# Two norms' row sums in one reciprocal: a windowed attention kernel on one Trainium2 core

## The chip, the cores and the metric

The kernel runs on one core of a Trainium2 chip. That core has a matrix engine (TensorE, PE in the profile), a vector engine (VectorE, DVE), an activation engine (ScalarE, ACT), a general engine (GpSimd, POOL) and SyncE (SP), which here only issues DMAs. The engines run at the same time and wait for one another through semaphores; each takes its own instructions in order. Matmuls write to PSUM, from which VectorE or ScalarE copy the result to SBUF. The metric is the device time of one execution in microseconds (us), and the median over several is compared.

## The reference

Two independent attention layers, A and B, of the same shape: 2048 tokens, width 1024, 32 heads of 32. Each query sees the 256 keys up to and including its own.

```python
def _A_ref(x, wqkv, wo):
    B, S, D = x.shape
    H = 32; Dh = D // H; W = 256
    qkv = (x @ wqkv).reshape(B, S, 3, H, Dh).transpose(2, 0, 3, 1, 4)
    q, k, v = qkv[0], qkv[1], qkv[2]
    scores = jnp.einsum("bhqd,bhkd->bhqk", q, k) * (Dh ** -0.5)
    idx = jnp.arange(S)
    mask = (idx[:, None] - idx[None, :] >= 0) & (idx[:, None] - idx[None, :] < W)
    p = softmax(jnp.where(mask[None, None], scores, -1e9), axis=-1)
    o = jnp.einsum("bhqk,bhkd->bhqd", p, v)
    return o.transpose(0, 2, 1, 3).reshape(B, S, D) @ wo
...
return jnp.concatenate([a, b], axis=-1)
```

All data are bf16 outside, sums are float32.

## The kernel before

**Tiling.** Tokens are cut into 16 blocks of 128 and 4 chunks of 512. Heads are taken in groups of four (128 columns), so there are 8 groups per problem and 16 in all, numbered `g`. For a key block j only the query blocks j, j+1 and j+2 matter, which makes 45 block pairs in a group. The list of all 16 x 45 pairs is cut into 180 *sessions* of four (L421).

**A session.** TensorE computes the transposed scores of four block pairs for four heads into one PSUM tile `st` (L434: four matmuls on 32-row tiles of the array at the same time). ACT takes one exponential over 128x2048 elements (L442) into `pt`. POOL zeroes the masked halves of the first and the last of the three blocks of a query (L450, L454). There is one `st`, so scores of the next session wait for the exponential.

**P·V and the norm.** For each group and each pair p of query blocks (8 per group, 128 in all) `pv` (L469) multiplies the exponentials with v and, with a matrix of ones, sums them over the keys. Four heads run beside each other on 32-column tiles of the array. Everything goes into one PSUM bank `acc` of 128 x 2 x 256 float32: half 0 is the product for two query blocks, half 1 the row sums, each repeated on the 32 rows of its head. For p > 0 VectorE has first added the two masked `pt` blocks of each query block into `both` (`edge`, L464), which saves row-sum matmuls: one burst of four 256-wide matmuls covers both query blocks' edges. The norm is three VectorE instructions that lie in the list `side`: two reciprocals of 128x128 (L505) and a multiplication of 128x256 (L510) that writes bf16 into `oT`. `acc` has two buffers.

**Projections.** `qk_steps`, `v_steps` and `out_steps` make *chains* of matmuls over eight 128-row tiles (`ct`) into one of two PSUM tiles `pp`, evacuated by ACT or VectorE (`evacuate`, L188). A chain of 8 or 16 matmuls has an earliest session (`early`), set among others by when its data are expected (`landed`), and a latest one (`late`). After the scores and the P·V of a session, `emit` issues steps of chains up to a budget that `level` spreads evenly over the sessions to come. Around P·V the projections run as four 32-column matmuls (L176) instead of one of 128 (L172), which spares a change of the array's tiling.

**Planner.** All this order is written out at build time. `_Clock` keeps estimated times of PE, ACT and VectorE; `COST` holds the estimates in ns with which `evacuate` chooses an engine and `emit` decides when to issue a piece of a norm. PE's order doesn't depend on `COST`.

**Loads.** Later weights and the x chunks of problem B are cut into pieces (L279 to L324). In each session, after a POOL mask that precedes it, a piece's destination is touched by a POOL memset of one column (L334) and its DMA issued on SP. A chunk of x comes in eight transposing DMAs of 128 tokens by 512 columns (L133). `arrival` records the session from which data count as there: that of the last piece plus two. For problem B, chunk k=2 is asked for from session 79, k=3 from 82; B's first scores are in session 90.

**Start.** The first 512 tokens come as four plain row loads on SP (L526), are transposed on PE (`flip`, L557) and copied by ACT and VectorE; the weights of q and k for group 0 are issued on ACT's queue (L528). POOL copies at L529 and L532 read row block 2 and write a column of `wv` and of x chunk 1, so those two loads on SP wait until that row block is in. Then come the weights of group 1, x chunks 2 and 3, and `wv` for groups 2 and 3.

**End.** The last output chain is evacuated 288 columns by ACT and 224 by VectorE, each with a DMA of its own (L257 to L260).

Of the kernel before, what the change touches and what calls it, by code (L numbers as in the profile page):

```python
# [8 lines left out]
BF16 = mybir.dt.bfloat16  # L9
F32 = mybir.dt.float32  # L10
# [3 lines left out]
ALU = mybir.AluOpType  # L14
# [4 lines left out]
P = 128  # L19
# [7 lines left out]
QB = 4  # L27
SLOTS = 4
VG = 2
NS_MM = 216.0  # L30
# [3 lines left out]
PV_LAG = 3  # L34
FREE = 10 ** 6
ACT_EXP = 1800.0
COST = {"act": 590.0, "dve": 670.0, "or": 560.0, "rinv": 930.0, "mult": 430.0,
        "edge": 340.0}


class _Cfg:
# [37 lines left out]
def _fast_path(ctx, tc, cfg, problems, outs, consts, certify):  # L79
    nc = tc.nc  # L80
# [30 lines left out]
    vp = ctx.enter_context(tc.tile_pool(name="vt", bufs=2 * NQ))  # L111
    ptp = ctx.enter_context(tc.tile_pool(name="pt", bufs=7))
    edgep = ctx.enter_context(tc.tile_pool(name="edge", bufs=2))
    misc = ctx.enter_context(tc.tile_pool(name="misc", bufs=2))
    osbp = ctx.enter_context(tc.tile_pool(name="osb", bufs=4))
    once = ctx.enter_context(tc.tile_pool(name="once", bufs=1))
    ps_st = ctx.enter_context(tc.tile_pool(name="ps_st", bufs=1, space=PSUM))
# [30 lines left out]
    def new_wv(m):  # L148
        wv[m] = wvp.tile([P, CT, VG * P], BF16, name="wv")
# [38 lines left out]
    def evacuate(out, in_, engines=("act", "dve")):  # L188
        if clock.evacuate(engines) == "act":
            nc.scalar.copy(out=out, in_=in_)  # L190
        else:
            nc.vector.tensor_copy(out=out, in_=in_)  # L192
# [23 lines left out]
    def v_steps(m, b):  # L216
# [19 lines left out]
                steps.append((NS_MM * w_ / 512.0, f))  # L236
        return steps

    def out_steps(pi, b, ch):
        k, a = divmod(b, QB)  # L240
        st_ = {}
        steps = []
        for ct in range(CT):
            def f(ct=ct):
                if ct == 0:
                    st_["pp"] = new_pp()
                by_columns(st_["pp"], 0, 512, oTs[(pi, k)][:, ct, a * P:(a + 1) * P],
                           wo_sb[(pi, ch)][:, ct, :], ct == 0, ct == CT - 1)
                clock.pe += NS_MM
                if ct == CT - 1:  # L250
                    osb = osbp.tile([P, 512], BF16, name="osb")
                    dst = outs[pi][b * P:(b + 1) * P, ch * 512:(ch + 1) * 512]
                    if chains or current:
                        evacuate(osb[:], st_["pp"][:])
                        nc.sync.dma_start(out=dst, in_=osb[:])
                    else:
                        nc.scalar.copy(out=osb[:, 0:288], in_=st_["pp"][:, 0:288])  # L257
                        nc.vector.tensor_copy(out=osb[:, 288:512], in_=st_["pp"][:, 288:512])
                        nc.scalar.dma_start(out=dst[:, 0:288], in_=osb[:, 0:288])
                        nc.sync.dma_start(out=dst[:, 288:512], in_=osb[:, 288:512])  # L260
            steps.append((NS_MM, f))
        return steps

# [45 lines left out]
    def entries_of(now):  # L309
        return [(n // NE,) + entries[n % NE]  # L310
                for n in range(now * SLOTS, min((now + 1) * SLOTS, G * NE))]

    pieces = {}
    arrival = {}
    free = 0
    for time, key, fs in wanted:
        free = max(free, time)
        new = fs[0]
        for where, f in fs[1:]:
            while len(pieces.get(free, [])) >= sum(q != j + 1 for _, j, q in entries_of(free)):  # L320
                free += 1
            pieces.setdefault(free, []).append((new, where, f))
            new = None
        arrival[key] = free + 2  # L324
# [29 lines left out]
    for pi in range(NPROB):  # L354
        final = pi == NPROB - 1
        for b in range(NB):
            k = b // QB
            for ch in range(cfg.NCH):
                early = max(pv_time(pi * T + T - 1, 2 * k + 1) + 1, landed("wo", pi, ch))
                late = FREE if final else wo_time[(pi + 1, ch)] - 1  # L360
                if not final and k < NPROB * NQ - (2 * NQ - 1):
                    late = pv_time((pi + 1) * T, 2 * (2 * NQ - 1 - NQ + k)) - 1
                chains.append(_Chain(early, late, out_steps(pi, b, ch)))
    assert all(c.early <= c.late for c in chains), [(c.early, c.late, c.size) for c in chains
                                                    if c.early > c.late]
    chains.sort(key=lambda c: c.late)
# [102 lines left out]
    def pv(g, p):  # L469
        pi, t = divmod(g, T)  # L470
        m, u = divmod(g, VG)
        k, h = divmod(p, QB // 2)
        segs = []
        for j in range(max(2 * p - 2, 0), 2 * p + 2):
            for q in range(max(j, 2 * p), min(j + 3, 2 * p + 2)):
                s, a = place(g, j, q)
                if segs and segs[-1][0] == j and segs[-1][2] == s:
                    segs[-1][4] += 1
                else:
                    segs.append([j, q, s, a, 1])  # L480
        acc = ps_acc.tile([P, 2, 256], F32, name="acc")
        clock.pe = max(clock.pe, clock.norms.pop(0))
        moves = [(0, j, (q - 2 * p) * P, n * P, pts[s][:, :, a:a + n, :])
                 for (j, q, s, a, n) in segs]
        for (j, q, s, a, n) in segs:
            for i in range(n):
                if p == 0 or q + i == j + 1:
                    moves.append((1, j, (q + i - 2 * p) * P, P, pts[s][:, :, a + i:a + i + 1, :]))
        if p:
            moves.append((1, 0, 0, 2 * P, edges.pop((g, p))))  # L490
        for x, (which, j, o, w_, src) in enumerate(moves):
            for r in range(4):
                c = u * P + 32 * r
                lhsT = ones[:, 0:32] if which else vts[(m, j // QB)][:, j % QB, c:c + 32]
                nc.tensor.matmul(acc[32 * r:32 * r + 32, which, o:o + w_], lhsT=lhsT,  # L495
                                 rhs=src[:, r, :, :], start=(x == 0), stop=(x == len(moves) - 1),
                                 tile_position=(0, 32 * r), skip_group_check=True)
            clock.pe += NS_PV * w_ / P
        if (pi, k) not in oTs:
            oTs[(pi, k)] = opool.tile([P, T, 512], BF16, name="oT")  # L500
        rinv = misc.tile([P, 256], F32, name="rinv")
        pieces = []
        for a in range(2):
            def f(a=a):
                nc.vector.reciprocal(out=rinv[:, a * P:(a + 1) * P],  # L505
                                     in_=acc[:, 1, a * P:(a + 1) * P])
            pieces.append((COST["rinv"], f, False))

        def f():
            nc.vector.tensor_tensor(out=oTs[(pi, k)][:, t, h * 256:(h + 1) * 256],  # L510
                                    in0=acc[:, 0, :], in1=rinv[:], op=ALU.mult)
        pieces.append((COST["mult"], f, True))
        n = max([i + 1 for i, x in enumerate(side) if x[2]], default=0)
        side[n:n] = pieces
# [7 lines left out]
    new_wqk(0)  # L522
    new_wv(0)
    xrow = [rows[:, 2 * a:2 * a + 2, :].rearrange("p t n -> p (t n)") for a in range(QB)]
    for a in range(QB):
        nc.sync.dma_start(out=xrow[a], in_=problems[0][0][a * P:(a + 1) * P, :])  # L526
    for which in range(2):
        load_wqk(0, which, nc.scalar)  # L528
    nc.gpsimd.tensor_copy(out=wv[0][:, 0, 0:1], in_=xrow[2][:, 0:1])  # L529
    load_wv(0, 0, CT, nc.sync)  # L530
    new_x(0, 1)
    nc.gpsimd.tensor_copy(out=xT[(0, 1)][:, 0, 0:1], in_=xrow[2][:, 0:1])  # L532
    load_x(0, 1)
    new_wqk(1)
    for which in range(2):
# [1 line left out]
    for k in range(2, NQ):  # L537
        new_x(0, k)
        load_x(0, k)
    new_wv(1)  # L540
    load_wv(1, 0, CT, nc.sync)

    warm = ps_proj.tile([P, 512], F32, name="pp")
    for _ in range(5):
        nc.tensor.matmul(warm[:], lhsT=blank[:, 0:P], rhs=blank[:, 0:512], start=True, stop=True)
    flips = [ps_acc.tile([P, 2, 256], F32, name="acc") for _ in range(2)]
    flips = [f[:].rearrange("p a q -> p (a q)") for f in flips]
    flips.append(ps_st.tile([P, 4, SLOTS, P], F32, name="st")[:, 0].rearrange("p a q -> p (a q)"))
    flips.append(None)
    held = [{}, {}]  # L550

    def flip(a):
        if a == 3:
            flips[a] = ps_acc.tile([P, 2, 256], F32, name="acc")[:].rearrange("p a q -> p (a q)")
        f = flips[a].bitcast(BF16).rearrange("p (ct q) -> p ct q", q=P)
        for ct in range(CT):
            nc.tensor.transpose(out=f[:, ct, :], in_=xrow[a][:, ct * P:(ct + 1) * P],  # L557
                                identity=ident[:])
        dst = xT[(0, 0)][:, :, a * P:(a + 1) * P]
        half = CT // 2  # L560
        nc.scalar.copy(out=dst[:, :half, :], in_=f[:, :half, :])
        nc.vector.tensor_copy(out=dst[:, half:, :], in_=f[:, half:, :])
# [170 lines left out]
def kernel(  # L733
# [16 lines left out]
    outs = [of[:, pi * D:(pi + 1) * D] for pi in range(len(problems))]  # L750

    cpool = ctx.enter_context(tc.tile_pool(name="consts", bufs=1))
    ones = cpool.tile([P, 32], BF16, name="ones")
    nc.vector.memset(ones[:], 1.0)
    ones1 = cpool.tile([P, 1], F32, name="ones1")
    nc.vector.memset(ones1[:], 1.0)
    pm = cpool.tile([P, 1], F32, name="pm")
# [65 lines left out]
```

## Time and profile before

| | |
|---|---|
| median of 8 executions | 617.99 us (612.51 to 620.76) |
| the profiled execution | 617.02 us |
| its span in the profile | 615.3 us |
| the largest groups: exponentials on ACT (L442) | 180 x 1878 ns |
| masks on POOL (L450, L454) | 480 x some 690 ns |
| edge adds on DVE (L464) | 224 x 628 ns |
| matmuls of PE: L176, L172, L495, L434 | 6156, 1037, 3696, 1488 |
| DMA moved | 35.4 MB, mean 58 GB/s |

The span runs from the first to the last instruction in the profile; the time of an execution holds a little around it (1.7 us here). In the profile, "busy" of PE is the union of matmul records whose ends are modelled, so the starts of matmuls say more than their lengths. An entry such as "<-PE acc L495 29.4" gives idle time of an engine and who ended it. PEclk is the granted clock of TensorE in tenths.

### The profile page before, as it was taken

Reading aid. Unit: us, or ns where it says so; the run is one execution under the profiler, and the core shown is the slowest. Engines: PE = TensorE matmul, PEld = TensorE weight load, DVE = VectorE, ACT = ScalarE, POOL = GpSimd, SP = SyncE. Lnnn points to the kernel's source line nnn. Section 1 sums busy time; section 2 is a strip of 40 time slices with the busy share of each in tenths; the row PEclk is TensorE's granted clock in tenths of the full one; section 3 lists DMA queues with packets and bytes.
Section 4 is the critical chain, followed back from the end, with each engine's and each line's share of the span. In section 5 each row is a group of like instructions: output and inputs, shape, how many; then the busy total and the mean of one; then the engine's idle time right before and its main releaser. Section 6 shows DMA issues by size and latency. Waiting matters only on the chain.

```text
span 615.3 us, 27586 instructions
## 1 busy us (share of the span) xinstructions
PE 600.7 (98%) x12416; PEld 343.9 (56%) x12416; DVE 507.9 (83%) x817; ACT 440.7 (72%) x372; POOL 321.8 (52%) x632
## 2 busy tenths in 40 slices
PE   7999999999999999989999999999999999999996
PEld 5465466556655656545556665745446564545442
DVE  1488989998999899969998999888998999899300
ACT  3677888788878888748777777777777778775332
POOL 0456665655566666536555556556556555555000
PEclk9999999999999999989999999999999999999999
DMA  8924110111004510534101010112012030114221
GB/s 205 206 64 113 38 37 3 36 38 38 3 20 96 110 25 8 84 86 107 37 14 37 27 38 2 37 37 79 12 31 61 2 107 20 54 45 131 69 78 64
DMA packets 86796, 35.40 MB, mean 58 GB/s; under 512 B 65680, under 2 KB 86160, under 8 KB 86672
## 3 DMA queue, kind: packets, MB, share of 16 engines
q1 hardware_dynamic: 84448, 32.97, 21.6%
q8 instruction: 99, 1.62, 1.1%
q10 hardware_dynamic: 2224, 0.60, 0.4%
q14 instruction: 25, 0.20, 0.1%
HBM read 17.83 MB, written 8.39 MB: 43 GB/s over the span
## 4 chain that ended last, share of the span: by engine, by line
PE 91%; DMA 3%; DVE 2%; SPq 1%; ACT 1%; issue 0%; POOL 0%; DVEq 0%; ACTq 0%
PE pp L176 42%; PE pp L172 27%; PE acc L495 13%; PE st L434 9%; DMA xT<-in_A_x_dram 1%; DMA oT<-in_A_x_dram 1%; SPq L133 1%; ACT pt L442 1%; DVE rinv L505 1%; DVE both L464 1%; DMA xT<-in_B_x_dram 0%; DVE top L184 0%; SPq L145 0%; SPq L526 0%; DVE osb L192 0%
## 5 line engine op out<-in xcount | busy, mean ns | idle before, releaser
L442 ACT ACTIVATE pt<-st 128x2048 bf16<-128x2048 f32 x180 | 338.1, 1878 | 80.3 <-PE st L434 63.6
L505 DVE RECIPROCAL rinv<-acc 128x128 f32<-128x128 f32 x256 | 227.1, 924 | 29.7 <-PE acc L495 29.4
L454 POOL TENSOR_SCALAR_AFFINE_SELECT pt<-pt 128x512 bf16<-128x512 bf16 x224 | 151.8, 678 | 148.7 <-ACT pt L442 148.7
L450 POOL TENSOR_SCALAR_AFFINE_SELECT pt<-pt 128x512 bf16<-128x512 bf16 x256 | 177.4, 694 | 87.7 <-ACT pt L442 86.9
L176 PE MATMUL pp<-xT,wqk 128*32 128x512 bf16 x2688 | 160.5, 379 | 0.0
L464 DVE TENSOR_TENSOR both<-pt 128x512 bf16<-128x512 bf16 x224 | 131.7, 628 | 0.0
L176 PEld LDWEIGHTS <-wqk 128*32 128x32 bf16 x2688 | 71.5, 97 | 54.9
L172 PE MATMUL pp<-xT,wqk 128*128 128x512 bf16 (+1 forms) x368 | 86.7, 380 | 5.1 <-POOL wv L334 3.2
L176 PE MATMUL pp<-wv,xT 128*32 128x256 bf16 x2548 | 78.6, 273 | 0.0
L434 PE MATMUL st<-qT,kT 32*128 32x384 bf16 (+2 forms) x1488 | 71.6, 269 | 0.0
L176 PEld LDWEIGHTS <-xT 128*32 128x32 bf16 x2548 | 68.2, 97 | 4.6
L495 PE MATMUL acc<-pt,vt 128*32 128x128 bf16 (+1 forms) x2160 | 63.3, 239 | 0.1
L172 PE MATMUL pp<-wo_sb,oT 128*128 128x512 bf16 x282 | 63.1, 379 | 0.0
L434 PEld LDWEIGHTS <-kT 32*128 32x128 bf16 x1488 | 22.2, 92 | 66.1 <-issue 65.6
L172 PEld LDWEIGHTS <-wqk 128*128 128x128 bf16 x368 | 34.5, 100 | 43.9 <-issue 13.6
L510 DVE TENSOR_TENSOR oT<-acc,rinv 128x256 bf16<-128x256 f32 x128 | 54.1, 423 | 3.7
L190 ACT CAST osb<-pp 128x512 bf16<-128x512 f32 x51 | 29.8, 585 | 38.1 <-PE pp L172 25.7
L176 PE MATMUL pp<-wo_sb,oT 128*32 128x512 bf16 x920 | 54.0, 379 | 0.0
L495 PEld LDWEIGHTS <-vt 128*32 128x32 bf16 x2160 | 35.9, 96 | 26.6 <-issue 24.7
L172 PE MATMUL pp<-wv,xT 128*128 128x256 bf16 x387 | 47.3, 273 | 0.3 <-ACT kT L190 0.2
L172 PEld LDWEIGHTS <-oT 128*128 128x128 bf16 x282 | 26.9, 98 | 32.6 <-issue 1.7
L190 ACT CAST qT<-pp 128x512 bf16<-128x512 f32 x47 | 27.5, 584 | 21.5 <-PE pp L172 11.1
(46 smaller groups left out, 363.7 us busy)
## 6 DMA issues: line engine op xcount, KB each, us to landing
out_dram<-osb SPq DMA_DIRECT2D x63, 128.0 KB, 1.7
wqk<-in_B_wqkv_dram SPq DMA_DIRECT2D x32, 128.0 KB, 2.7
wqk<-in_A_wqkv_dram SPq DMA_DIRECT2D x24, 128.0 KB, 2.6
wo_sb<-in_A_wo_dram SPq DMA_DIRECT2D x16, 128.0 KB, 2.2
wv<-in_B_wqkv_dram SPq DMA_DIRECT2D x16, 128.0 KB, 2.5
wo_sb<-in_B_wo_dram SPq DMA_DIRECT2D x16, 128.0 KB, 2.3
oT<-in_A_x_dram SPq DMA_DIRECT2D x4, 256.0 KB, 5.1
wv<-in_A_wqkv_dram SPq DMA_DIRECT2D x2, 512.0 KB, 4.0
```

Of the source, the lines that this page charges most:

```text
L133: nc.sync.dma_start_transpose(out=xT[(pi, k)][:, c0:c1, lo:hi], in_=problems[pi][0][k * 512 + lo:k * 512 + hi, c0 * P:c1 * P])
L172: nc.tensor.matmul(out[:, lo:hi], lhsT=lhsT, rhs=rhs, start=start, stop=stop, skip_group_check=True)
L176: nc.tensor.matmul(out[c:c + 32, lo:hi], lhsT=lhsT[:, c:c + 32], rhs=rhs, start=start, stop=stop, tile_position=(0, c), skip_group_check=True)
L190: nc.scalar.copy(out=out, in_=in_)
L434: nc.tensor.matmul(st[:, r, a:b, :], lhsT=kT[32 * r:32 * r + 32, j * P:(j + 1) * P], rhs=qT[32 * r:32 * r + 32, q * P:(q + b - a) * P], st ...
L442: nc.scalar.activation(out=pt[:, :, :n, :].rearrange("p r a q -> p r (a q)"), in_=st[:, :, :n, :].rearrange("p r a q -> p r (a q)"), func= ...
L450: nc.gpsimd.affine_select(out=blk, in_=blk, pattern=[[0, 4], [1, P]], compare_op=ALU.is_ge, fill=0.0, base=0, channel_multiplier=-1)
L454: nc.gpsimd.affine_select(out=blk, in_=blk, pattern=[[0, 4], [-1, P]], compare_op=ALU.is_gt, fill=0.0, base=0, channel_multiplier=1)
L464: nc.vector.tensor_tensor(out=both[:, :, h, :], in0=pts[s0][:, :, a0, :], in1=pts[s1][:, :, a1, :], op=ALU.add)
L495: nc.tensor.matmul(acc[32 * r:32 * r + 32, which, o:o + w_], lhsT=lhsT, rhs=src[:, r, :, :], start=(x == 0), stop=(x == len(moves) - 1), t ...
L505: nc.vector.reciprocal(out=rinv[:, a * P:(a + 1) * P], in_=acc[:, 1, a * P:(a + 1) * P])
L510: nc.vector.tensor_tensor(out=oTs[(pi, k)][:, t, h * 256:(h + 1) * 256], in0=acc[:, 0, :], in1=rinv[:], op=ALU.mult)
```

## The change

1. **Row sums stacked.** `ones` becomes two 128x32 matrices: the first has ones in columns 0 to 15, the second in 16 to 31, zeros elsewhere. The sums of the pair's first query block then land on rows 0 to 15 of each head's 32, those of the second on 16 to 31, in the same 128 columns. `acc` is 128x512, of which 384 columns are used. The burst on `both` is split in two, one for each query block.
2. **The norm.** One reciprocal of 128x128; then two stream shuffles that copy row 0 or row 16 of each 32 to all 32 rows, into the two halves of `wide`; then the multiplication as before, with `wide`. Shuffles and multiplication are one piece. `rinv` and `wide` have one buffer each.
3. **Planner.** `COST` of "mult" and "edge" is raised. Of an x chunk at most two pieces go into a session. The loads of the start are entered in `arrival`: x chunks 2 and 3 count from sessions 3 and 5, q/k weights of group 1 from 1, `wv` of groups 2 and 3 from 4.
4. **First loads.** On SP: row blocks 0 and 1, k's weights, row blocks 2 and 3, `wv`, x chunk 1, and so on; q's weights alone stay on ACT's queue. Both POOL copies go. The second `wv` is issued ahead of x chunk 3.
5. **End.** The last chain is computed and stored in two halves of 256 columns, each in its own `pp` and with one evacuation and one DMA on SP.

```diff
-COST = {... "rinv": 930.0, "mult": 430.0, "edge": 340.0}
+COST = {... "rinv": 930.0, "mult": 900.0, "edge": 620.0}
...
-    misc = ctx.enter_context(tc.tile_pool(name="misc", bufs=2))
+    normp = ctx.enter_context(tc.tile_pool(name="norm", bufs=1))
...
+    def store(pi, b, ch, lo, hi, pp):
+        osb = osbp.tile([P, 512], BF16, name="osb")
+        evacuate(osb[:, lo:hi], pp[:, lo:hi])
+        nc.sync.dma_start(out=outs[pi][b * P:(b + 1) * P, ch * 512 + lo:ch * 512 + hi],
+                          in_=osb[:, lo:hi])
+
+    def last_steps(pi, b, ch):
...
+        for lo in (0, 256):
+            for ct in range(CT):
+                def f(ct=ct, lo=lo):
+                    if ct == 0:
+                        st_["pp"] = new_pp()
+                    by_columns(st_["pp"], lo, lo + 256, oTs[(pi, k)][:, ct, a * P:(a + 1) * P],
+                               wo_sb[(pi, ch)][:, ct, lo:lo + 256], ct == 0, ct == CT - 1)
+                    clock.pe += NS_MM / 2
+                    if ct == CT - 1:
+                        store(pi, b, ch, lo, lo + 256, st_["pp"])
...
-                    osb = osbp.tile([P, 512], BF16, name="osb")
-                    dst = outs[pi][b * P:(b + 1) * P, ch * 512:(ch + 1) * 512]
-                    if chains or current:
-                        evacuate(osb[:], st_["pp"][:])
-                        nc.sync.dma_start(out=dst, in_=osb[:])
-                    else:
-                        nc.scalar.copy(out=osb[:, 0:288], in_=st_["pp"][:, 0:288])
-                        nc.vector.tensor_copy(out=osb[:, 288:512], in_=st_["pp"][:, 288:512])
-                        nc.scalar.dma_start(out=dst[:, 0:288], in_=osb[:, 0:288])
-                        nc.sync.dma_start(out=dst[:, 288:512], in_=osb[:, 288:512])
+                    store(pi, b, ch, 0, 512, st_["pp"])
...
-    arrival = {}
+    arrival = {("x", 0, k): t for k, t in ((2, 3), (3, 5))}
+    arrival.update({("wqk", 1): 1, ("wv", 1): 4})
...
-            while len(pieces.get(free, [])) >= sum(q != j + 1 for _, j, q in entries_of(free)):
+            while len(pieces.get(free, [])) >= min(2 if key[0] == "x" else SLOTS, sum(
+                    q != j + 1 for _, j, q in entries_of(free))):
                 free += 1
...
-        acc = ps_acc.tile([P, 2, 256], F32, name="acc")
+        acc = ps_acc.tile([P, 512], F32, name="acc")
...
                 if p == 0 or q + i == j + 1:
-                    moves.append((1, j, (q + i - 2 * p) * P, P, pts[s][:, :, a + i:a + i + 1, :]))
+                    moves.append((q + i - 2 * p, j, 2 * P, P, pts[s][:, :, a + i:a + i + 1, :]))
         if p:
-            moves.append((1, 0, 0, 2 * P, edges.pop((g, p))))
+            both = edges.pop((g, p))
+            moves += [(h, 0, 2 * P, P, both[:, :, h:h + 1, :]) for h in range(2)]
...
-                lhsT = ones[:, 0:32] if which else vts[(m, j // QB)][:, j % QB, c:c + 32]
+                lhsT = vts[(m, j // QB)][:, j % QB, c:c + 32] if h is None else ones[:, h, :]
...
-        for a in range(2):
-            def f(a=a):
-                nc.vector.reciprocal(out=rinv[:, a * P:(a + 1) * P],
-                                     in_=acc[:, 1, a * P:(a + 1) * P])
-            pieces.append((COST["rinv"], f, False))
 
         def f():
-            nc.vector.tensor_tensor(out=oTs[(pi, k)][:, t, h * 256:(h + 1) * 256],
-                                    in0=acc[:, 0, :], in1=rinv[:], op=ALU.mult)
+            nc.vector.reciprocal(out=rinv[:], in_=acc[:, 2 * P:3 * P])
+        pieces.append((COST["rinv"], f, False))
+
+        def f():
+            for h in range(2):
+                nc.vector.stream_shuffle(out=wide[:, h * P:(h + 1) * P], in_=rinv[:],
+                                         mask=[16 * h] * 32)
+            nc.vector.tensor_tensor(out=oTs[(pi, k)][:, t, (p % 2) * 256:(p % 2 + 1) * 256],
+                                    in0=acc[:, 0:256], in1=wide[:], op=ALU.mult)
         pieces.append((COST["mult"], f, True))
...
+    load_wqk(0, 0, nc.scalar)
     for a in range(QB):
         nc.sync.dma_start(out=xrow[a], in_=problems[0][0][a * P:(a + 1) * P, :])
-    for which in range(2):
-        load_wqk(0, which, nc.scalar)
-    nc.gpsimd.tensor_copy(out=wv[0][:, 0, 0:1], in_=xrow[2][:, 0:1])
+        if a == 1:
+            load_wqk(0, 1, nc.sync)
     load_wv(0, 0, CT, nc.sync)
     new_x(0, 1)
-    nc.gpsimd.tensor_copy(out=xT[(0, 1)][:, 0, 0:1], in_=xrow[2][:, 0:1])
     load_x(0, 1)
...
         load_x(0, k)
-    new_wv(1)
-    load_wv(1, 0, CT, nc.sync)
+        if k == 2:
+            new_wv(1)
+            load_wv(1, 0, CT, nc.sync)
...
-    ones = cpool.tile([P, 32], BF16, name="ones")
-    nc.vector.memset(ones[:], 1.0)
+    ones = cpool.tile([P, 2, 32], BF16, name="ones")
+    nc.vector.memset(ones[:], 0.0)
+    nc.vector.memset(ones[:, 0, 0:16], 1.0)
+    nc.vector.memset(ones[:, 1, 16:32], 1.0)
```

## The prediction

> **What bounds the kernel now.** I read the page first: span, busy shares, the slices, the chain.
>
> ```profile
> span 615.3 us, 27586 instructions
> PE 600.7 (98%) x12416; PEld 343.9 (56%) x12416; DVE 507.9 (83%) x817; ACT 440.7 (72%) x372; POOL 321.8 (52%) x632
> ...
> PEclk9999999999999999989999999999999999999999
> ...
> PE 91%; DMA 3%; DVE 2%; SPq 1%; ACT 1%; issue 0%; POOL 0%; DVEq 0%; ACTq 0%
> ```
>
> TensorE is busy or on the chain nearly always, at full clock but for one slice. Busy time alone doesn't prove it streams, so I took the starts of all its matmuls and compared each spacing with columns/2.4 ns plus a few ns. All excess together is 44.5 us: 37 us are pauses of 0.1 us where the shape of the array tile changes (two per session, not touched by the change); most of the rest lies at three places below. Seven other spacings of 0.14 to 0.35 us over sum to 1.6 us.
>
> VectorE is the engine to be relieved. The table of windows, for the stretch in which norms run (its columns: window, us, then busy us of PE, PEld, DVE, ACT, POOL), then the groups and the waits:
>
> ```profile
> 25.00:576.00 551.00, 546.88 (x12117) 316.02 (x12116) 501.69 (x802) 418.20 (x341) 316.67 (x618) 1.00 0.20 50
> L505 DVE RECIPROCAL rinv<-acc 128x128 f32<-128x128 f32 x256 | 227.1, 924 | 29.7 <-PE acc L495 29.4
> L510 DVE TENSOR_TENSOR oT<-acc,rinv 128x256 bf16<-128x256 f32 x128 | 54.1, 423 | 3.7
> PEld L495 <- DVE oT L510: 0.6, 2, 0.3
> ```
>
> VectorE is 91% busy there, but it is VectorE that waits for PE (29.4 us), while PE waits for a norm 0.6 us in all. Work taken from VectorE is work taken from an engine that is not last.
>
> **Norms on VectorE.** Removed: one reciprocal in each of 128 norms, 924 ns. Added: two shuffles of 128x128 f32 with a mask that alternates. The trace has no shuffle. Nearest row is L510: 423 ns for 256 elements, of which 256/0.96 = 267 ns stream (one element a cycle, if the clock is the 0.96 GHz of the Trainium skill's "Trainium Kernel Development and Optimization", NeuronCore Architecture), leaving 156 ns fixed. So 128 elements: 133 + 156 = 290 ns. The skill's "VectorE: DVE Perf Modes", The perf-mode tier table, gives about 2400 ns for 2048 elements with no faster mode, hence 267 ns fixed and 400 ns here; no run here shows one. Loading the mask has no row: between 0 and 0.15 us, an estimate (one more fixed part). Ends: 290 to 550 ns per shuffle. I take 350, by the row it is nearest to: 2x350 - 924 = -224 ns per norm, 29 us off VectorE (ends: -44 and +23 us). The same skill page, Rules for kernel authors, says to minimize the count of chained operations, which speaks against trading one for two; by row or rule the new pair costs about or under the old reciprocal. **To the span: nothing** in any of these cases, since PE's streaming hides it. That cover ends where the pair exceeds 924 ns plus the slack per norm, (551 - 502)/128 = 385 ns: at 0.65 us each.
>
> The norm's pieces go from three to two and `acc` comes free sooner; its wait is only 0.6 us.
>
> **Row sums on PE.** For p > 0 (112 of 128) one burst of four 256-wide matmuls on `both` becomes two bursts of 128. A rule speaks against it: "TensorEngine Tiling (Array Packing)", Instruction Overhead, puts about 60 cycles on each matmul; 448 more at 60/2.4 = 25 ns would be 11 us. The timeline (start, length):
>
> ```profile
> 302.80 0.28 PE L495 MATMUL acc<-pt,ones 128*32 128x128 bf16 x8
> 302.91 0.28 PE L495 MATMUL acc<-both,ones 128*32 128x256 bf16 x4
> 303.02 0.39 PE L176 MATMUL pp<-wo_sb,oT 128*32 128x512 bf16 x4
> ```
>
> Two bursts of 128 take 302.80 to 302.91, one of 256 takes 302.91 to 303.02: the same 0.11 us. Weight loads are hidden. From start to start the records have 56 ns for a burst of 128 and 109 ns for one of 256, so 3 ns per split: **+0.3 us** (0.2 to 1.1, the latter if a whole hundredth is lost each time). The wider zero/one weights cost nothing more: still 32 columns. Two more memsets at the start (about 0.1 us each by the ones row, 85 ns) delay the warm-up matmuls, which end at 3.6 while the first transposes wait for data until 4.5.
>
> **First loads.** SP issues x rows 0, 1, then k's weights (from ACT's queue), rows 2, 3, `wv`, and x chunk 1 without the two POOL copies that held SP from 2.6 to 8.08; `wv` of group 1 passes x chunk 3. PE's start hangs on row 2 (transposes at 7.86). Before it must land three rows and both weights either way, 1.28 MB over the same DMA engines: I take **0** (-0.6 to +0.9, the latter if row 2 really waits for k's 256 KB at some 290 GB/s). What moves is x chunk 2, for which PE stops:
>
> ```profile
> 22.11 0.61 PE L172 MATMUL pp<-xT,wqk 128*128 128x512 bf16 x2
> ...
> 24.05 2.10 PE L172 MATMUL pp<-xT,wqk 128*128 128x512 bf16 x9 [1.34 <-DMA xT<-in_A_x_dram]
> ```
>
> 24.05 - 22.33 - 0.216 = 1.5 us. Its transpose was issued at 14.91. Now: SP's six plain loads to about 3.5, chunk 1's transpose 5.1 to 6.5 us, two weights 1.2, so issue near 10.5 and landing near 19, ahead of session 3, from which the planner now uses it (about 26). Chunk 3, passed by one load of 0.58 us, lands near 25, against session 5 (31.8). Sessions 0 to 2 have q, k of group 1 and v in its place. **-1.5 us** (-1 to -2).
>
> **The x chunks of problem B.** This is the largest wait:
>
> ```profile
> 250.30 12.73 SPq L133 DMA_TRANSPOSE xT<-in_B_x_dram  x8
> ...
> 259.82 0.39 PE L172 MATMUL pp<-xT,wqk 128*128 128x512 bf16 x1
> ...
> 263.44 1.02 PE L172 MATMUL pp<-xT,wqk 128*128 128x512 bf16 x4 [3.23 <-POOL wv L334]
> ...
> 264.85 3.15 PE L172 MATMUL pp<-xT,wqk 128*128 128x512 bf16 x7 [0.39 <-DMA xT<-in_B_x_dram]
> ```
>
> Eight transposes of chunk 2 take SP 1.6 us each, so the last two end at 261.7 and 263.0 and land some 1.7 us later, although the planner counted them in for session 83 (scores at 259.49). PE stands 3.4 and 0.55 us, then takes 0.43 us per matmul instead of 0.216, its clock having dropped: about 5.6 us in all. (The page names POOL; the chain of waits names the DMA.) With at most two x pieces per session the eight fill sessions 79 to 82 instead of 79 to 81, so this chunk counts as there from 84, not 83. What is available before is spread over one more session, about 0.75 us of PE work less by session 79, so the issues begin some 0.7 us sooner; SP stays their limit, and they land near 262 and 263.5. PE gets to the chain one session's scores and P·V later: 260.0 + 1.1 = 261.1. Left are stalls of about 1 and 0.5 us, too short to cool the clock (the 1.5 us at 22.33 didn't): 1.5 to 2 instead of 5.6, **-3.6 us** (-1 to -5). Chunk 3 counts from 90, not 88; its chains are due at 97. Chunks 0 and 1 and a `wv` come one to three sessions later and aren't needed before session 80.
>
> **Costs in the planner.** Per norm with its edges VectorE is charged 930+900+2x620 = 3070 ns, before 2x930+430+2x340 = 2970: the split of evacuations hardly moves, and the true load now lies at or below the charge. **0** (+-1).
>
> **The tail.**
>
> ```profile
> 609.74 0.40 ACT L257 CAST osb<-pp 128x288 bf16<-128x288 f32 x1 [1.14 <-PE pp L172]
> ...
> 610.16 0.39 DVE L258 CAST osb<-pp 128x224 bf16<-128x224 f32 x1 [34.60 <-ACT osb L257]
> 610.59 0.33 SPq L260 DMA_DIRECT2D out_dram<-osb  x1
> ```
>
> VectorE's half waits for ACT's, so the last DMA is issued at 610.59. Now the first half is evacuated under the second half's matmuls, and the second takes one cast of 256 columns, about 0.37 us: issue near 610.13. **-0.45 us** (-0.2 to -0.7); eight more matmuls cost 0.03.
>
> **Sum.** 0.3 - 1.5 - 3.6 - 0.45 = -5.25. The profiled execution took 617.02, its span 615.3 and 1.7 around it: 610.05 and 611.8. The median shown, 617.99, lies 1 us above that execution, so I forecast 612.7.
>
> **Rivals.** About 0.5% (3.1 us) is what a measurement here can tell from no change.
> - *A, as above* (0.66): 612.7, from 611 to 614.9.
> - *B, transposes stay late* (0.17): SP's issue rate is unchanged, and if it slips, chunk 2's wait only moves to session 84. For: nearly all of those 12.7 us are issue. Against: PE comes 1.1 us later on any reading. Then 618.0 + 0.3 - 1.5 - 0.45 = 616.4.
> - *C, VectorE was pacing* (0.07): a lighter VectorE also removes the seven small waits, 1.6 us: 611.1. Against: the one that the trace names (0.19 us at 78.41) follows ACT.
> - *D, the shuffle pair is dear* (0.10): mask reloads and SBUF contention (the edge adds on `both` average 628 ns for 512 elements) put each above 0.65 us. VectorE then sets the pace: at 0.75 us, (1500 - 1309) x 128 = 24 us, less 5: 637; it cancels the gains at 0.68 us. Against: more than twice the nearest row.
>
> That the change doesn't do what it says is excluded for the reciprocal: 128 rows by 128 columns instead of twice that.
>
> **Chances.** Faster: A and C, less a little of A's upper edge, 0.70. Same: 0.19, B with that edge. Slower: D and accidents, 0.11. The range, 609.8 to 617.3, holds A, B and C with their costs.
>
> **What would show it.** Reciprocals x128 at about 924 ns; shuffles x256 at 290 to 400; VectorE near 480 us busy and PE's waits for it still under 1 us; no wait for A's x near 22 us; the wait near 260 under 2 us with the clock held; the last DMA about 0.45 us after its matmuls. I am wrong if PE stops between bursts for `acc` or `pp`, or if that wait keeps its 3 us.

## The result, and the profile after

The changed kernel takes 612.42 us in the median (611.32 to 614.23, 22 executions); the kernel before, timed beside it, 616.51 us (612.51 to 623.51, 59 executions). The ratio is 0.9932, with a 95% interval from 0.9918 to 0.9945: about 4.2 us faster. The profiled execution took 613.37 us and spans 611.6.

The page of the changed kernel: span, busy shares, clock, chain of waits, and the groups of the norm.

```profile
span 611.6 us, 28789 instructions
PE 600.6 (98%) x12824; PEld 345.7 (57%) x12824; DVE 464.0 (76%) x1193; ACT 445.3 (73%) x382; POOL 328.9 (54%) x630
...
PEclk9999999999999999999999999999999999999999
...
PE 95%; ACT 2%; DMA 1%; issue 0%; SPq 0%; POOL 0%; ACTq 0%
...
L524 DVE RECIPROCAL rinv<-acc 128x128 f32<-128x128 f32 x128 | 121.9, 953 | 56.3 <-PE acc L513 55.9
L481 DVE TENSOR_TENSOR both<-pt 128x512 bf16<-128x512 bf16 x224 | 138.4, 658 | 0.0
...
L529 DVE STREAM_SHUFFLE wide<-rinv 128x128 f32<-128x128 f32 x256 | 64.6, 298 | 0.0
...
L531 DVE TENSOR_TENSOR oT<-acc,wide 128x256 bf16<-128x256 f32 x128 | 54.4, 425 | 4.4
```

VectorE lost 44 us of busy time (507.9 to 464.0), and the span fell by 3.7. Some 37 us of the 44 are the norm itself; with its higher charge the planner also gave nine evacuations to ACT (VectorE has 60 instead of 69). Its waiting for PE's row sums grew from 29.4 to 55.9 us: more than half of what was taken from it became idle time. In the chain, PE's share rose from 91 to 95% and that of DMA fell from 3 to 1%. The places of two waits of before, in the timeline; the later one with SP's issues:

```profile
22.82 0.60 PE L172 MATMUL pp<-xT,wqk 128*128 128x512 bf16 x2
...
23.26 2.13 PE L172 MATMUL pp<-wv,xT 128*128 128x256 bf16 x18
...
250.21 12.10 SPq L133 DMA_TRANSPOSE xT<-in_B_x_dram  x8
...
262.60 1.05 PE L176 MATMUL pp<-xT,wqk 128*32 128x512 bf16 x16 [0.57 <-DVE both L481]
...
263.99 1.48 PE L176 MATMUL pp<-xT,wqk 128*32 128x512 bf16 x24 [0.34 <-DMA xT<-in_B_x_dram]
```

At 23 us a v chain stands where q of x chunk 2 had waited. Chunk 2 of A's x landed at 21.74 us. Near 262 us the starts of matmuls are 0.73 and 0.51 us late, 1.25 us in place of 5.6, and the clock stays up. SP needs the same 12 us for its eight transposes: they were not made faster, PE comes to them later.

One pair of profiles doesn't give the sizes, though. The kernel before scatters over 11 us, the changed one over 3. So each part was timed on its own, and two of them, the norm and the limit on x pieces, were also taken out of the changed kernel.

### The profile page after: what moved, and what is told of

Its sections match the earlier page's. It is cut to its first block, busy times and chain, and to the rows that moved or that the text cites. A ratio compares the mean times of both kernels' runs of the same rounds, so it can differ in the third digit from the quotient of the medians.

```text
span 611.6 us, 28789 instructions
## 1 busy us (share of the span) xinstructions
PE 600.6 (98%) x12824; PEld 345.7 (57%) x12824; DVE 464.0 (76%) x1193; ACT 445.3 (73%) x382; POOL 328.9 (54%) x630
## 4 chain that ended last, share of the span: by engine, by line
PE 95%; ACT 2%; DMA 1%; issue 0%; SPq 0%; POOL 0%; ACTq 0%
PE pp L176 43%; PE pp L172 29%; PE acc L513 13%; PE st L451 10%; ACT pt L459 2%; DMA oT<-in_A_x_dram 1%; DMA xT<-in_B_x_dram 0%; ACT vt L190 0%; PE st L578 0%; ACT kT L190 0%; PE acc L578 0%; SPq L548 0%; POOL pt L471 0%; ACT qT L190 0%; SPq L145 0%
## 5 line engine op out<-in xcount | busy, mean ns | idle before, releaser
L471 POOL TENSOR_SCALAR_AFFINE_SELECT pt<-pt 128x512 bf16<-128x512 bf16 x224 | 156.4, 698 | 144.7 <-ACT pt L459 144.7
L467 POOL TENSOR_SCALAR_AFFINE_SELECT pt<-pt 128x512 bf16<-128x512 bf16 x256 | 180.0, 705 | 88.1 <-ACT pt L459 88.1
L524 DVE RECIPROCAL rinv<-acc 128x128 f32<-128x128 f32 x128 | 121.9, 953 | 56.3 <-PE acc L513 55.9
L481 DVE TENSOR_TENSOR both<-pt 128x512 bf16<-128x512 bf16 x224 | 138.4, 658 | 0.0
L176 PEld LDWEIGHTS <-xT 128*32 128x32 bf16 x2436 | 63.7, 97 | 5.2
L529 DVE STREAM_SHUFFLE wide<-rinv 128x128 f32<-128x128 f32 x256 | 64.6, 298 | 0.0
L172 PE MATMUL pp<-wo_sb,oT 128*128 128x512 bf16 (+1 forms) x288 | 62.4, 373 | 0.0
L190 ACT CAST osb<-pp 128x512 bf16<-128x512 f32 (+1 forms) x54 | 31.2, 577 | 38.3 <-PE pp L172 26.9
L531 DVE TENSOR_TENSOR oT<-acc,wide 128x256 bf16<-128x256 f32 x128 | 54.4, 425 | 4.4
L172 PE MATMUL pp<-wv,xT 128*128 128x256 bf16 x415 | 51.0, 273 | 0.4 <-ACT kT L190 0.2
L172 PEld LDWEIGHTS <-xT 128*128 128x128 bf16 x415 | 38.9, 98 | 11.6 <-issue 5.1
```

What stands on the lines that cost most here:

```text
L172: nc.tensor.matmul(out[:, lo:hi], lhsT=lhsT, rhs=rhs, start=start, stop=stop, skip_group_check=True)
L176: nc.tensor.matmul(out[c:c + 32, lo:hi], lhsT=lhsT[:, c:c + 32], rhs=rhs, start=start, stop=stop, tile_position=(0, c), skip_group_check=True)
L467: nc.gpsimd.affine_select(out=blk, in_=blk, pattern=[[0, 4], [1, P]], compare_op=ALU.is_ge, fill=0.0, base=0, channel_multiplier=-1)
L471: nc.gpsimd.affine_select(out=blk, in_=blk, pattern=[[0, 4], [-1, P]], compare_op=ALU.is_gt, fill=0.0, base=0, channel_multiplier=1)
L481: nc.vector.tensor_tensor(out=both[:, :, h, :], in0=pts[s0][:, :, a0, :], in1=pts[s1][:, :, a1, :], op=ALU.add)
L524: nc.vector.reciprocal(out=rinv[:], in_=acc[:, 2 * P:3 * P])
```

## The experiments

Theory W: the time is made of PE's matmuls and its waits for loads, and the stacked norm moves nothing. Theory V: VectorE's relief is what pays. The runs were timed in three groups, each on one chip with the kernel before beside it: first the four `b_` runs; then `a_nostack`, `a_shuf2`, `a_warm` and `a_x4`; last `after_again`, `a_nostack_again`, `a_nocap` and `a_warm_x4`. The kernel before took 617.70, 615.55 and 618.42 us in them, so times are compared within a group.

**One part alone: two x pieces per session** (`b_xcap`).

```diff
-            while len(pieces.get(free, [])) >= sum(q != j + 1 for _, j, q in entries_of(free)):
+            while len(pieces.get(free, [])) >= min(2 if key[0] == "x" else SLOTS, sum(
+                    q != j + 1 for _, j, q in entries_of(free))):
```

> The kernel before with one edit alone: at most two pieces of an x chunk in a session. Theory W (the gain is made of waits of PE for data): the wait near 260 us shrinks from 5.6 us to about 1.3 us, the clock stays up, and the time falls by about 4 us (3 to 5), a ratio near 0.9935. Theory V (the gain comes from the relief of VectorE): no change, within 1 us, since VectorE does the same work here.

Measured: 616.41 us beside 617.70, ratio 0.9982 (0.9954 to 1.0011). PE's timeline:

```profile
263.29 1.05 PE L176 MATMUL pp<-xT,wqk 128*32 128x512 bf16 x16 [0.17 <-issue]
266.40 1.48 PE L176 MATMUL pp<-xT,wqk 128*32 128x512 bf16 x24 [2.06 <-DMA xT<-in_B_x_dram]
```

From start to start of matmuls PE was 0.34 and 2.23 us late, twice the 1.3 us expected, and the clock held; no 4 us came of it. The wait at 22 us is still there (2.06 us in this profile), and the times scatter by 5 us; the interval runs from 2.8 us faster to 0.7 slower. What the limit is worth isn't settled by this run; `a_nocap`, below, measures it in the changed kernel.

**One part alone: the first loads** (`b_loads`: the hunk of the start and the entries of `arrival`, as in the change).

> The kernel before with the new first loads and the entries of the start in arrival, nothing else. Theory W: the wait of 1.5 us at 22 us goes; session 0 begins at 16.1 us if its later start in the changed kernel (16.85) was chance, or again 0.7 us later if the new order of loads causes it. So the time falls by 1.5 us in the first case and by 0.8 us in the second. Theory V: no change.

Measured: 614.76 us, ratio 0.9946 (0.9924 to 0.9969), so 3.3 us: twice what theory W had. Session 0 began at 16.48 us, in between. The expected 1.5 us was the wait in one profile. Profiles of other kernels with the old loads show that it can be longer. The timeline of PE in `b_stack`, then in `b_tail`:

```profile
21.99 0.60 PE L172 MATMUL pp<-xT,wqk 128*128 128x512 bf16 x2
24.58 3.60 PE L172 MATMUL pp<-xT,wqk 128*128 128x512 bf16 x9 [1.99 <-DMA xT<-in_A_x_dram]
28.11 0.53 PE L434 MATMUL st<-qT,kT 32*128 32x384 bf16 x8
```

```profile
17.24 0.81 PE L172 MATMUL pp<-xT,wqk 128*128 128x512 bf16 x2 [1.21 <-DMA xT<-in_A_x_dram]
...
23.17 2.10 PE L172 MATMUL pp<-xT,wqk 128*128 128x512 bf16 x9 [1.44 <-DMA xT<-in_A_x_dram]
```

In the first the stall is 2.15 us (from matmul to matmul) and the clock drops at 25.0 us: nine matmuls take 3.60 us instead of 2.10. In the second, whose clock rose early, chunk 1 is waited for as well, 1.4 us, and chunk 2 again 1.6 us. So the loads of before had no margin: in these profiles a stall there cost between 1.5 and some 3.7 us, the 3.7 with the half clock. That such stalls make up the 3.3 us fits, but the share of executions with each isn't known.

**One part alone: the tail** (`b_tail`: `store` and `last_steps`, as in the change).

> The kernel before with the last output chain in two halves, nothing else. The last DMA is issued 0.45 us sooner after the last matmul. If its landing takes as long as before (2.45 us from issue to the wait's end), the time falls by 0.4 us; if it takes 3.06 us again as in the changed kernel, the gain is given back and the time stays within 0.2 us.

Measured: 617.65 us, ratio 1.001 (0.9977 to 1.0042): nothing that this comparison can see. In the records the last DMA is issued 0.64 us after the last matmul has streamed instead of 1.09, as expected. From that issue to its landing it took 3.04 us. In the profile of before this was 2.66 us (the expectation's 2.45 us is the wait for the other half's DMA), but that was a short one: the other three profiles with the old tail have 3.09 to 3.25 us. Beside those the 0.45 us stand, too small to be told from times that scatter by 8 us.

**One part alone: the stacked norm** (`b_stack`: `ones`, `acc`, the norm and `COST`, as in the change).

> The kernel before with the stacked row sums, the single reciprocal, the shuffles and the new costs of the planner, nothing else. Theory W: VectorE's busy time falls by some 40 us and the time doesn't: 0 to +0.5 us (112 split bursts, 0.3 us), unless evacuations now come at worse moments, which would add up to 1 us. Theory V: the time falls by 2 us or more.

Measured: 616.38 us, ratio 0.9967 (0.9945 to 0.999); VectorE 463.7 us busy. This looked like theory V, 2 us. So norm and `COST` together were taken out of the changed kernel, whose times scatter less (theory V2: the stacked norm is worth 2 us by itself):

```diff
-        acc = ps_acc.tile([P, 512], F32, name="acc")
+        acc = ps_acc.tile([P, 2, 256], F32, name="acc")
...
-        def f():
-            nc.vector.reciprocal(out=rinv[:], in_=acc[:, 2 * P:3 * P])
-        pieces.append((COST["rinv"], f, False))
+        for a in range(2):
+            def f(a=a):
+                nc.vector.reciprocal(out=rinv[:, a * P:(a + 1) * P],
+                                     in_=acc[:, 1, a * P:(a + 1) * P])
+            pieces.append((COST["rinv"], f, False))
```

> The changed kernel with the old norm (two reciprocals, unstacked sums, the old costs of the planner); loads, x cap and tail stay new. Theory W (waits for loads alone): VectorE goes back to about 500 us busy and the time stays within 0.5 us of the changed kernel, a ratio to before of 0.993. Theory V2 (the stacked norm is worth 2 us by itself, as its run alone suggests): about 2 us slower than the changed kernel, a ratio of 0.996 to 0.997.

> The changed kernel with the old norm once more, now beside the changed kernel on the same chip. Theory W: within 0.7 us of it. Theory V2: 2 us slower.

> The changed kernel as it is, for comparison with the three beside it on one chip: a ratio of 0.993 to before.

Measured: 612.06 us in the second group, ratio 0.9942 (0.9919 to 0.9965). In the third 612.56, ratio 0.9913 (0.9891 to 0.9935), beside the changed kernel's 612.91, ratio 0.9912 (0.9891 to 0.9932). The busy shares of `a_nostack`:

```profile
PE 599.9 (98%) x12376; PEld 344.7 (56%) x12376; DVE 506.2 (83%) x811; ACT 443.5 (73%) x378; POOL 323.5 (53%) x630
```

The same time with VectorE at 506 us busy as at 464. For the changed kernel theory V2 falls. The 2 us of `b_stack`, with an interval of 0.6 to 3.4 us, stay unexplained: its profile still has the waits for both loads (2.15 us at 24.6 and the clock's drop behind it, 2.4 and 0.7 us near 265), and their scatter may have made the 2 us, but that isn't shown.

**More work on VectorE** (`a_shuf2`).

```diff
             for h in range(2):
-                nc.vector.stream_shuffle(out=wide[:, h * P:(h + 1) * P], in_=rinv[:],
-                                         mask=[16 * h] * 32)
+                for _ in range(2):
+                    nc.vector.stream_shuffle(out=wide[:, h * P:(h + 1) * P], in_=rinv[:],
+                                             mask=[16 * h] * 32)
```

> The changed kernel with each shuffle issued twice: VectorE gets about 0.6 us more per norm, 75 us in all, more than the stacking took from it, with PE's order and the planner as they are. By the slack (some 0.7 us per norm) it fits beneath PE. Theory W: no change, within 0.5 us of the changed kernel. Theory V: the gain is lost and more, 4 us or more slower.

Measured: 619.83 us, ratio 1.0067 (1.0044 to 1.009): 7.8 us slower than `a_nostack` beside it. Theory W's number was wrong here. The table of windows of `a_nostack`, then of `a_shuf2` (window, us, busy us of PE, PEld, DVE, ACT, POOL), with the latter's chain and waits:

```profile
25.00:570.00 545.00, 543.57 (x12050) 314.02 (x12043) 499.81 (x796) 419.83 (x345) 318.87 (x619) 1.00 0.19 49
```

```profile
25.00:570.00 545.00, 538.65 (x12339) 311.26 (x12340) 504.90 (x1660) 420.10 (x347) 309.71 (x619) 1.00 0.20 48
```

```profile
PE 70%; DVE 23%; issue 3%; ACT 1%; DMA 1%; POOL 1%; SPq 0%; DVEq 0%; ACTq 0%
...
L530 DVE STREAM_SHUFFLE wide<-rinv 128x128 f32<-128x128 f32 x512 | 140.6, 297 | 0.0
...
L481 DVE TENSOR_TENSOR both<-pt 128x512 bf16<-128x512 bf16 x224 | 113.3, 546 | 0.0
...
L530 DVE LOAD_MASK_SELECT wide<-rinv x512 | 7.2, 14 | 15.6
```

```profile
ACT pt L459 <- DVE wide L530: 5.0, 7, 1.2
...
PE acc L513 <- DVE both L481: 0.9, 2, 0.5
PE pp L172 <- DVE vt L192: 0.9, 3, 0.4
```

Busy time hardly tells the two apart, 500 and 505 us of 545; but 15.6 us of idle time lie before the mask loads, so VectorE was held for some 520 us. At 92% it cost nothing, at about 95% PE waits for edge sums and evacuations, and a quarter of the chain runs over VectorE. Between 18 us and the last output chains the starts of matmuls have 21 delays of more than 0.13 us, 9.9 us together, of which 5.3 us are put down to VectorE; the changed kernel has 10, 3.7 us together. The difference of 6.2 us is that of the two spans (617.7 and 611.6).

Busy time hides the added work for another reason too. The shuffles took 76 us more, but the edge adds 25 us less: 546 ns each instead of 658. By overlap of the records, an edge add beside which no mask of POOL runs takes 411 to 414 ns, one with a mask beside it for more than a third of its time some 750 ns. In `a_shuf2` 119 of the 224 have no mask beside them, in the changed kernel 57.

Part of the 7.8 us may come from the planner, which doesn't know of the added work and still gives VectorE evacuations; that wasn't separated. VectorE's margin was there before the change, but thin; the stacking widens it.

**The cap taken out** (`a_nocap`: the edit of `b_xcap` undone in the changed kernel).

> The changed kernel without the limit of two x pieces per session. By the prediction's size of that step it is 3.6 us slower than the changed kernel. By the runs of single parts (the limit alone moved 1.1 us, and everything but limit, stacking and tail left 0.9 us to the changed kernel) it is about 1 us slower: the wait near 260 us is 3 to 4 us again, but the waits for evacuations near 187, 199 and 231 us (1.4 us together) are shorter without the limit.

Measured: 615.53 us, ratio 0.9942 (0.9919 to 0.9965), beside 612.91: 2.6 us slower, between the two expectations. Two of its seven executions (612.56 and 613.30 us) are about as fast as the changed kernel, the other five took 615.1 to 616.0 us: the stall seems not to come in every execution. The timeline of PE:

```profile
257.79 0.40 PE L450 MATMUL st<-qT,kT 32*128 32x128 bf16 x8
261.69 4.85 PE L172 MATMUL pp<-xT,wqk 128*128 128x512 bf16 x11 [3.50 <-POOL wv L349]
266.48 0.61 PE L450 MATMUL st<-qT,kT 32*128 32x384 bf16 x8
```

The stall is back with 3.4 us (the weights of a twelfth matmul, ahead of it, are loaded at 258.12; its own record is missing), and the eleven after it take 4.85 us instead of 2.55, at half clock. That is some 5.7 us at this place. What the cap gives back elsewhere is seen in the changed kernel's timeline:

```profile
187.60 0.59 PE L172 MATMUL pp<-xT,wqk 128*128 128x512 bf16 x2 [0.30 <-ACT vt L190]
...
232.00 0.59 PE L172 MATMUL pp<-xT,wqk 128*128 128x512 bf16 x2 [0.39 <-ACT kT L190]
```

By the starts of matmuls, PE is 0.46, 0.36 and 0.55 us late at 187, 199 and 231 us, for evacuations on ACT; both profiles of the changed kernel have all three, and the one without the cap has none. The cap changes which chains end in which session, and these end badly: 5.7 us against the changed kernel's 1.2 here and 1.4 elsewhere is 3.1 us, as the spans of the two profiles differ (614.1 and 611.1).

**Two additions to the changed kernel.** Dummy matmuls in the pauses of the start (`a_warm`; `dummies` writes the unused tile of the warm-up, which had five matmuls before):

```diff
+    dummies(6, 512)
...
     flip(0)
+    dummies(3, 256)
     flip(1)
+    dummies(3, 256)
     flip(2)
```

> The changed kernel with dummy matmuls in the pauses between the first transposes, so that PE is busy from 1.3 us on. If the clock at the start is granted after a stretch of dense work, it is up by about 8 us in every execution instead of at 11 to 14 us, session 0 begins about 2 us sooner (near 14.5 us) and the time falls by 2 us, a ratio of 0.990 to before. If x chunk 1 then lands too late, a wait near 16 us takes part of it back. If the moment of the clock doesn't hang on such work: no change.

Measured: 610.08 us, ratio 0.991 (0.9887 to 0.9933), 2.0 us below `a_nostack` beside it. The 24 matmuls after the last transposes, in the changed kernel and in `a_warm`:

```profile
11.21 3.96 PE L172 MATMUL pp<-xT,wqk 128*128 128x256 bf16 x24
```

```profile
9.25 2.78 PE L172 MATMUL pp<-xT,wqk 128*128 128x256 bf16 x24
...
13.71 0.40 PE L451 MATMUL st<-qT,kT 32*128 32x384 bf16 x8
```

They run at full clock from the first. The clock is granted at 5.9 us, where the changed kernel had it at 13.6, and session 0 begins at 13.71 us instead of 16.85. Chunk 1 of x was there in time (13.39 us). The edit adds a sixth warm-up matmul and fills the pauses; which of the two brings the clock sooner wasn't separated.

Wider transposes (`a_x4`):

```diff
-                for c in range(0, CT, 4):
-                    fs.append((lambda pi=pi, k=k, a=a, c=c: xT[(pi, k)][:, c, a * P:a * P + 1],
-                               lambda pi=pi, k=k, a=a, c=c: load_x(pi, k, a, 1, c, c + 4)))
+                fs.append((lambda pi=pi, k=k, a=a: xT[(pi, k)][:, 0, a * P:a * P + 1],
+                           lambda pi=pi, k=k, a=a: load_x(pi, k, a, 1)))
```

> The changed kernel with the x chunks of problem B in four transposing DMAs of 128 tokens by 1024 columns instead of eight by 512. Theory S (SP's issue of these DMAs is the limit of the wait near 260 us): issue of a whole chunk takes 6 to 8 us instead of 12, the rest of that wait (1.3 us) goes, and the time falls by about 1 us, a ratio of 0.9915. If an issue takes twice as long for twice the columns: no change.

Measured: 610.61 us, ratio 0.9913 (0.989 to 0.9937), 1.5 us below `a_nostack`. SP's issues in the timeline:

```profile
249.55 6.26 SPq L133 DMA_TRANSPOSE xT<-in_B_x_dram  x4
```

A chunk takes 6.3 us of SP instead of 12.1: by its single issues 1.26 us for twice the columns. Of the wait near 260 us 0.4 us are left, and the three late evacuations are gone, as the pieces again fall in other sessions. So not all of the 1.5 us need be theory S.

Both together (`a_warm_x4`):

> The changed kernel with both the dummy matmuls of the start and the four wide transposes per chunk. If the two gains are in different places they add: about 4 us faster than the changed kernel, 608.5 us or a ratio near 0.987 to before.

Measured: 609.83 us, ratio 0.9856 (0.9832 to 0.988), 3.1 us below the changed kernel beside it, where 4 were expected. The sum is incomplete: in this profile PE waits again for chunks 2 and 3 of B's x, 0.74 us each. It is the fastest version measured here.

## Why the prediction was right

It named 612.7 us, and 612.42 were measured. The mechanism held: PE bounds, and the gain is waits for loads that went. But the nearness to 0.3 us is in part luck. The forecast was a fall of 5.25 us from 617.99, the median of eight executions. Over the 59 beside the changed kernel that median is 616.51, and the fall is about 4.2 us (5.5 in the last group, from 618.42). A start 1.5 us too high and a fall about 1 us too large nearly cancel.

- **What bounds.** Right, and shown by `a_nostack`: 42 us more or less on VectorE leave the time where it is.
- **The norm.** A shuffle takes 298 ns. The row of L510 had said 290, the estimate from the Trainium skill's "VectorE: DVE Perf Modes", The perf-mode tier table, 400; the row was right, and the choice of 350 too high. The mask load, put between 0 and 150 ns, is 14 ns busy and some 20 ns of idle time before it. Worth nothing in time, as forecast. The cover was judged too generously: the prediction let it last until 0.65 us per shuffle, the slack being counted as idle time of VectorE per norm. The four shuffles of `a_shuf2` with their mask loads and gaps come to 1.28 us per norm, as much as a pair at 0.64 us each, just under that limit, and it cost over 7 us, where the prediction still had none. Idle time on average isn't idle time where PE needs the evacuation.
- **Row sums on PE.** Right: by the starts of matmuls the row sums of `both` last 109 or 110 ns before and 111 or 112 ns after, in 110 of the 112 bursts of each profile. That is 3 ns a burst, 0.3 us in all. In the times it can't be told from nothing. The 11 us by the Trainium skill's "TensorEngine Tiling (Array Packing)", Instruction Overhead, are excluded by both.
- **First loads.** Mis-sized: -1.5 us forecast, -3.3 measured alone. The step took the stall of one profile for the stall of the kernel. In other profiles with the old loads it lasted up to 2.15 us, took the clock down, or met chunk 1 too. The new loads came later than forecast, chunk 2 issued at 12.96 us and landed at 21.74 instead of 10.5 and 19, since chunk 1's transpose held SP for 7.9 us; session 3 was late enough for that. For the start itself zero was about right: with the clock granted late, session 0 begins at 15.8 to 17.1 us with the new loads and at 16.0 to 16.2 with the old ones.
- **x chunks of B.** The mechanism was right in its parts: same issue time, the last two pieces landed at 262.4 and 263.7 us, PE later by a session, stalls of 0.7 and 0.5 us instead of 1 and 0.5, clock held. That such stalls leave the clock up rested on one stall of 1.5 us; in `b_loads` one of 1.6 us, with one of 0.65 behind it, took it down. The term, -3.6 us, measured 2.6 (`a_nocap`). Missing were the late evacuations at other places, 1.4 us, which come from the moved chains; the prediction has no term for them, and "Costs in the planner" stands at 0.
- **The tail.** -0.45 us from the end of the last matmul to the issue: 0.64 instead of 1.09 us in the records, just that. In the times it is below what can be told.
- **Rivals.** B falls with the smaller wait. C falls: the small waits became longer, not shorter (1.6 us before, 2.4 after). D didn't come about, the shuffle being at the row's price, but its point of decision lies nearer than written.

Within the fall too, errors cancel in part: the loads gave 1.8 us more than forecast, the x chunks 1.0 us less. The two measured sizes add up to 5.9 us, more than the fall of 4.2 or 5.5; each has an error of more than a microsecond, and they come from different groups, so the sum isn't closed.

## What to carry to other kernels

Before a faster instruction is credited with time, find out who waits for whom: here 44 us off an engine that was 91% busy gave nothing that could be told in the changed kernel, and the order of loads gave the gain. The size of a stall for a DMA can't be read from one profile; here the kernels with the old loads scattered most, and parts are best measured by taking them out of the version that scatters least. A stall that takes the clock down is paid for twice: in `a_nocap` 3.4 us, and 2.3 more at half clock.

## What was not expected of the hardware

- **The clock at the start.** In eleven of the twelve profiled executions with the five warm-up matmuls, then pauses of 0.4 to 1.3 us until the third block's transposes, full clock was granted at 11.3 to 13.9 us; in one (`b_tail`) at 5.2 us, although its matmuls up to 6 us start within 0.03 us of the changed kernel's, where it came at 13.6. With a sixth warm-up matmul and the pauses filled it came at 5.9 and 4.6 us, and session 0 began at 13.7 and 14.6 us instead of 15.8 to 17.1 us. What decides the moment stays open.
- **The clock in a stall.** Stalls of 1.5, 2.06, 2.22, 2.23 and 2.4 us left it up; others of 1.6 (with one of 0.65 soon after), 2.15, 2.4 and 3.4 us took it to half, for 3.4 us or, in `a_nocap`, 6.8 us. The length alone doesn't decide near 2 us.
- **Transposing DMAs.** An issue on SP takes 1.22 us for 128 tokens by 512 columns and 1.26 us for 1024, in the median; some take 1.5 to 2.8 us.
